# Pooled attention and MLP-mixer on one core: batch 0 is prepared in the way of the other batches

## The chip, the cores and the metric

The kernel runs on one core of one Trainium2 chip. Such a core has TensorE (matmuls, called PE in the profile; its weight loads are PEld), VectorE (DVE), ScalarE (ACT), GpSimd (POOL) and SyncE (SP); each works through its own list of instructions in order, and waits on semaphores where it needs what another one makes. Sixteen DMA engines move data between the chip's memory and the core's. The metric is the device time of one execution in microseconds (us); the median of several runs counts.

## What is computed

The reference, cut to what matters:

```python
# q, k, v: (8 batches, 8 heads, 576 rows, 64); x below is attention's output as (8, 576, 512)
k_p = k.reshape(B, H, 72, 8, D).mean(axis=3)          # keys pooled by 8 rows
v_p = v.reshape(B, H, 72, 8, D).mean(axis=3)          # values too
scores = (1 / sqrt(D)) * q @ k_p.transpose(0, 1, 3, 2)
attn = softmax(scores, axis=-1)
x = attn @ v_p                                        # heads side by side in 512 columns

h = relu(x.transpose(0, 2, 1) @ w_tok1) @ w_tok2      # 576 -> 256 -> 576
u = x + h.transpose(0, 2, 1)
out = u + relu(u @ w_ch1) @ w_ch2                     # 512 -> 1536 -> 512
```

All eight batches use the same weights. Inputs and output are fp32.

## The kernel before, in words

**Order.** Nothing is left to a scheduler: the whole program is recorded under `tc.manual_schedule`, and the order in which Python calls the steps is the order of instructions on every engine. Two texts at the top hold that order. `HEAD` is a list of tokens that are run first: loads (`L...`), dummy matmuls on a zeroed tile that feed nothing (`d4` is four of them), the attention of batch 0, and the first steps of batch 1. `PLAN` has one dictionary for each of nine units. A unit is the channel MLP of one batch (units 0 to 7; unit 8 takes the left-over rows of all batches): 12 tiles of the first product (`l1_tile`, lines L515 to L522, two steps each) and then seven products of 12 matmuls (L583, three steps each), whose sums and differences of operands (`=1` to `=4`, `w0` to `w3`, L545 and L557) are made by DVE. Between its steps `PLAN` puts the attention and token mixing of the next batches: `2.s0` is step `s0` of batch 2, `5.lq` a load of batch 5's queries, `g` a gate: a DVE memset and a POOL copy of one number (L716, L717) that keeps POOL from running ahead of that place.

**PSUM.** `take` and `give` hand out four one-bank tiles (p1a to p1d) in the order in which they come free. The pool `ps_two` has two tiles of two banks that are used in turn: a tile can be written again when the instruction that reads it has ended.

**A batch 1 to 7.** Its queries come with one POOL DMA as bf16, four heads on the 128 partitions, 18 rows of queries to a partition (`load_q`, L126). `qD` (steps `Q0`, `Q1`, L281) turns them on DVE by 32 x 32 blocks. Keys and values come with 72 partitions in use, eight rows to be pooled side by side (`kv`, L117). Keys are pooled by three adds (`pool8`, L171) on POOL, for batch 1 by eight accumulating matmuls with the identity (`kpool`, L250), and turned by four transposes on TensorE and a copy on ACT (`kpT`, L219). `scores` (L291, steps `s0` to `s2`) makes scores with 32-row matmuls on four row groups of the array at a time, into both `ps_two` tiles, and two exps on ACT. `av` (L372) multiplies with the values and normalizes on DVE (L383, L384); `at`, `u` and `t` are the token mixing.

**Batch 0** has steps of its own in `HEAD`. Queries of heads 0 to 3 come as fp32 with two SP DMAs (L742) and are cast by ACT and DVE (`c0`, `c1`, L694), those of heads 4 to 7 come with a POOL DMA (`Lq`, L700), 9 rows to a partition. `q0` to `q3` (`qT`, L272) turn two heads each by five transposes on TensorE and a DVE copy. Keys come with three POOL DMAs (`LkA`, `LkT`, `LkB`: heads 0 to 3, the last eight partitions, heads 4 to 7). `kp0` to `kp2` (`kp2`, L227) pool them by matmuls with the identity, DVE copies the sums into a zeroed tile (`kpz`), and `kt0` to `kt2` (`kt2`, L238) turn them, once for even and once for odd blocks of rows. `o0` to `o3` and `e0` to `e3` (`score`, L309) make the scores of two heads with full 128-row matmuls, one `ps_two` tile and one exp each. Then `vpool0` and `vpool1` (L259) pool the values on TensorE, `a00` to `a14` (`avh`, L325) multiply four heads with them and normalize on DVE (L338, L339), `m00` to `m14` (`ath`, L347) are the first product of the token mixing in two halves of columns, whose relu is one ACT instruction for the first half and an ACT and a DVE one for the second (L362, L364, L365), and `X0` to `X3` and `A0` to `A3` (L464, L472) make batch 0's turned input of the channel MLP. `1.kpool` pools batch 1's keys, `p0` and `p1` permute a weight (L159).

## Time and profile before

| | |
|---|---|
| runs of the kernel | 264.4, 265.07, 265.51 us; median 265.07 |
| the execution that was profiled | 264.03 us |
| its span, first to last instruction | 262.2 us |
| TensorE busy | 255.8 us (98%) |
| DVE, ACT, POOL busy | 179.7, 119.2, 150.0 us |
| TensorE, 0 to 6.55 / 6.55 to 13.10 / 13.10 to 24.10 us | 5.36 / 5.60 / 10.90 us busy |
| granted TensorE clock | 1.00 in the whole span |

How to read it: the profile gives each engine's instructions with their start and duration. A line such as `L517 PE MATMUL p1d<-uT,w_ch 128*128 128x512` is an instruction of line 517 on TensorE with 128 rows and 128 columns of weights, that writes tile p1d, 512 columns wide, from uT and w_ch. What stands in brackets or after `<-` behind it is the idle time of the engine before it, and what ended that. In the waits, the three numbers are us in total, how often, and the longest. Matmuls overlap each other, so their durations are longer than the time from one start to the next; 512 columns take 0.216 us from start to start. DMA landings are the start of the issue plus the time to landing that the trace gives.

### The profile page before, as it was taken

To read this page: it belongs to the slowest core of one execution; us is meant where nothing else is said; L and a number is where in the kernel's file an instruction comes from. 1 tells how busy PE (TensorE), PEld (TensorE's weight loads), DVE (VectorE), ACT (ScalarE), POOL (GpSimd) and SP (SyncE) were. 2 spreads that over 40 slices of the span, in tenths; PEclk is the share of its full clock that TensorE was granted. 3 is DMA by queue.
4 is the path that set the end of the run, shared out by engine and by line. 5 is a ranking of instruction groups with operands and counts; after the bars stand their busy time and mean duration, and the time that the engine had idled before them with its cause. 6 is when DMAs were issued, how large, how long until landed. Compare 5 with 4: busy or idle time off the path is not lost.

```text
span 262.2 us, 5324 instructions
## 1 busy us (share of the span) xinstructions
PE 255.8 (98%) x2121; PEld 160.4 (61%) x2121; DVE 179.7 (69%) x370; ACT 119.2 (45%) x195; POOL 150.0 (57%) x177
## 2 busy tenths in 40 slices
PE   8899999999999999999999999999999999999994
PEld 3775556754658545864487448744774486486483
DVE  4566489998786657993899449964795486175183
ACT  2445754149465554435641584155535502612610
POOL 8576145999989999999939881988000000101000
PEclk9999999999999999999999999999999999999999
DMA  7999999992096839699357840831414054503204
GB/s 150 191 200 205 206 206 208 207 223 77 2 172 101 133 118 201 146 196 261 66 154 125 239 133 2 162 92 41 123 35 127 5 158 113 129 0 88 75 0 160
DMA packets 31704, 34.29 MB, mean 131 GB/s; under 512 B 3136, under 2 KB 23744, under 8 KB 31680
## 3 DMA queue, kind: packets, MB, share of 16 engines
q0 software_dynamic: 17632, 17.64, 42.6%
q1 hardware_dynamic: 13632, 15.93, 20.4%
q10 hardware_dynamic: 416, 0.39, 0.5%
q8 instruction: 16, 0.26, 0.4%
q14 instruction: 8, 0.07, 0.1%
HBM read 38.99 MB, written 12.58 MB: 197 GB/s over the span
## 4 chain that ended last, share of the span: by engine, by line
PE 80%; POOL 8%; DMA 7%; DVE 3%; issue 1%; POOLq 0%
PE p1d L517 9%; PE p1c L517 9%; PE p1a L517 8%; PE p1b L517 7%; PE p1b L583 7%; PE p1c L583 7%; PE p1a L583 6%; DMA qb<-in_q_dram 5%; PE p1d L583 4%; PE p L297 3%; PE p L379 3%; POOL t L174 2%; POOL t L175 2%; DMA kr<-in_k_dram 2%; PE p L583 2%; PE p1d L393 2%
## 5 line engine op out<-in xcount | busy, mean ns | idle before, releaser
L717 POOL COPY flag<-flag 1x1 f32<-1x1 f32 x47 | 12.6, 269 | 94.5 <-DVE flag L716 94.5
L517 PEld LDWEIGHTS <-w_ch 128*128 128x128 bf16 x432 | 39.6, 98 | 43.4 <-issue 1.8
L583 PEld LDWEIGHTS <-area 128*128 128x128 bf16 x432 | 40.9, 98 | 7.4 <-issue 1.2
L306 ACT ACTIVATE ex<-p 72x768 bf16<-72x768 f32 x42 | 31.6, 803 | 15.9 <-PE p L297 15.7
L583 PEld LDWEIGHTS <-GT 128*128 128x128 bf16 x324 | 30.8, 98 | 8.2 <-issue 2.4
L175 POOL TENSOR_TENSOR t<-t 72x512 f32<-72x512 f32 x23 | 31.0, 1346 | 1.8
L521 ACT ACTIVATE GT<-p1d 128x512 bf16<-128x512 f32 x29 | 17.3, 597 | 27.0 <-PE p1d L517 21.4
L517 PE MATMUL p1d<-uT,w_ch 128*128 128x512 bf16 x104 | 28.8, 379 | 0.0
L174 POOL TENSOR_TENSOR t<-kr 72x1024 f32<-72x1024 bf16 x12 | 25.9, 2155 | 0.5
L517 PE MATMUL p1c<-uT,w_ch 128*128 128x512 bf16 x96 | 26.1, 379 | 0.0
L521 ACT ACTIVATE GT<-p1b 128x512 bf16<-128x512 f32 x26 | 15.6, 598 | 23.2 <-PE p1b L517 16.8
L517 PE MATMUL p1a<-uT,w_ch 128*128 128x512 bf16 x92 | 25.3, 379 | 0.0
L517 PE MATMUL p1b<-uT,w_ch 128*128 128x512 bf16 x92 | 24.2, 379 | 0.0
L174 POOL TENSOR_TENSOR t<-vr 72x1024 f32<-72x1024 bf16 x11 | 24.1, 2187 | 0.3
L521 ACT ACTIVATE GT<-p1a 128x512 bf16<-128x512 f32 x26 | 15.5, 596 | 11.8 <-PE p1a L517 9.2
L521 ACT ACTIVATE GT<-p1c 128x512 bf16<-128x512 f32 x27 | 16.1, 598 | 8.7 <-PE p1c L517 8.3
L384 DVE TENSOR_TENSOR x<-p,den 128x512 bf16<-128x512 f32 x28 | 19.4, 692 | 1.0
L557 DVE TENSOR_TENSOR area<-GT 128x1536 bf16<-128x1536 bf16 x9 | 9.8, 1086 | 12.4 <-ACT GT L521 12.4
L545 DVE TENSOR_TENSOR area<-GT 128x1536 bf16<-128x1536 bf16 x9 | 10.6, 1178 | 10.1 <-ACT GT L521 7.7
L379 PEld LDWEIGHTS <-ex 72*128 72x128 bf16 x280 | 13.4, 98 | 5.6 <-DVE flag L716 0.4
L583 PE MATMUL p1c<-area,area 128*128 128x256 bf16 x120 | 15.4, 273 | 0.0
L379 PE MATMUL p<-vp,ex 72*128 72x65 bf16 x280 | 14.6, 194 | 0.0
(188 smaller groups left out, 461.1 us busy)
## 6 DMA issues: line engine op xcount, KB each, us to landing
out_dram<-o SPq DMA_DIRECT2D x32, 256.0 KB, 4.0
qb<-in_q_dram POOLq DMA_DIRECT2D x7, 576.0 KB, 9.3
kr<-in_k_dram POOLq DMA_DIRECT2D x7, 512.0 KB, 7.4
vr<-in_v_dram POOLq DMA_DIRECT2D x7, 512.0 KB, 9.8
w_ch<-in_moe_w_ch_dram POOLq DMA_DIRECT2D x5, 512.0 KB, 15.8
mem<-u SPq DMA_DIRECT2D x10, 256.0 KB, 2.0
v<-mem SPq DMA_DIRECT2D x20, 128.0 KB, 2.8
area<-in_q_dram SPq DMA_DIRECT2D x2, 288.0 KB, 3.0
```

What stands on the lines that cost most here:

```text
L174: eng.tensor_tensor(out=t4[:, 0:n], in0=t[:, hs, 0:4], in1=t[:, hs, 4:8], op=ALU.add)
L175: eng.tensor_tensor(out=t4[:, 0:n, 0:2], in0=t4[:, 0:n, 0:2], in1=t4[:, 0:n, 2:4], op=ALU.add)
L297: nc.tensor.matmul(out=pss[l // 2][0:SP, l % 2, o:o + n1 - n0], lhsT=st["kD"][quad, g, db, :], rhs=st["qD"][quad, g, n0:n1, db], start=(db ...
L306: nc.scalar.activation(out=dst, in_=src, func=AF.Exp, scale=scale)
L379: nc.tensor.matmul(out=ps[:, h // 4, (h % 4) * (D + 1):(h % 4 + 1) * (D + 1)], lhsT=st["ex"][:, h * S + n0:h * S + n0 + P], rhs=st["vp"][: ...
L384: nc.vector.tensor_tensor(out=dst.rearrange("p (a h d) -> p a h d", a=2, d=D), in0=view[:, :, :, 0:D], in1=den[rows, :, :, None].broadcast ...
L517: nc.tensor.matmul(out=ps, lhsT=w_ch1[:, kk, m * P:(m + 1) * P], rhs=uT[kk], start=(kk == 0), stop=(kk == 3))
L521: nc.scalar.activation(out=GT[:, m, :], in_=ps, func=AF.Relu)
L545: nc.vector.tensor_tensor(out=out, in0=a, in1=b, op=ALU.subtract)
L557: nc.vector.tensor_tensor(out=S4[:, 0], in0=GT[:, f, hi], in1=GT[:, sec, hi], op=ALU.add)
L583: nc.tensor.matmul(out=ps[i] if split else ps[:, i], lhsT=chunk(u, i, a(m)), rhs=w(m), start=start and m == 0 and (i == 0 or split), stop= ...
L717: nc.gpsimd.tensor_copy(out=flag[:, 1:2], in_=flag[:, 0:1])
```

## The change

Batch 0 drops its own way and takes that of the other batches. Its queries all come by POOL, four heads to a DMA (`Lqa`, `Lqb`), and are turned by DVE (`Q0`, `Q1`). The keys of heads 0 to 3 come as fp32 by the SP queue (two DMAs, 64 and 8 partitions) into `kf` and are pooled by three DVE adds (`k0`); those of heads 4 to 7 come by POOL (`LkT` now has only these heads, `LkB` as before), are pooled by matmuls and copied by DVE (`kp2`). Each half is turned by two transposes and an ACT copy (`h0`, `h1`). Scores are `s0` to `s2`. Casts, `qT`, `kt2`, `score` and two memsets go. `HEAD` and `PLAN` are written anew; every unit keeps its kinds of matmuls, while places of steps, loads and gates differ.

```diff
-HEAD = """LkA LkT LkB Lq LvA LvT LvB Lt1 Lk1 Lt2 Lc1a Lq1 Lc1b Lc1c Lv1 Lc2b Lc1d p1 Lc2a Lc2c d4 c0 prep d3 c1 d4 d2 d1 q0 d2 kp0 kp1 kt0 q1 kt1 o0 kp2 o1 q3 e1 kt2 e0 q2 e3 vpool0 o3 d1 d1 a00 e2 vpool1 o2 a02 m01 d1 a04 m00 a12 m03 X1 m02 a10 m04 X0 p0 a14 1.kpool m11 m12 m14 m13 m10 A1 X3 A0 X2 A2 A3"""
+HEAD = """Lqa LkT LkB Lqb LvT LvA LvB Lt1 Lk1 Lt2 Lc1b Lc1a Lq1 Lc1c Lv1 Lc1d p1 Lc2a Lc2b Lc2c prep d4 d2 d3 k0 d3 d2 d4 h0 Q0 s0 kp2 Q1 h1 s1 vpool0 s2 vpool1 a00 a02 a04 m01 m00 X0 a10 X1 m03 m02 a12 m04 p0 1.kpool m10 m12 a14 m13 A1 X3 m11 m14 A0 X2 A2 A3"""
...
-    {2: "3.av4", 3: "3.av0 4.K0", 7: "3.av1", 8: "g 4.K1", 10: "3.av2 3.av3", 13: "g 3.at0", 14: "3.at1 g 6.lk", 16: "4.kpT", 17: "=3", 18: "4.Q0 3.u2", 19: "3.u1", 20: "3.u0", 21: "3.M0", 22: "3.u3 4.s2", 23: "3.M2 4.V1 3.u4", 24: "4.V0", 25: "=1", 26: "=2 3.M4", 27: "4.s0 g", 28: "6.lq", 30: "=4 g", 31: "4.s1 5.lv", 34: "3.M g", 35: "4.av2 3.T1", 36: "3.MT", 38: "3.T2", 40: "3.T3 3.T0", 41: "4.av4", 44: "5.lq 3.T5"},
...
+    {1: "4.K1", 2: "3.av4", 3: "3.av0", 7: "3.av2", 9: "4.K0", 10: "g 3.av1", 11: "3.av3", 12: "g =3", 14: "6.lk 3.at1", 15: "3.at0 g", 16: "4.Q0", 17: "4.V0 4.kpT", 18: "3.u1 3.u3", 20: "3.u0 4.V1", 21: "3.u2 4.s2", 22: "3.u4 3.M0", 24: "=1 3.M2", 25: "g 5.lq", 26: "=2", 27: "3.M4 4.s1", 28: "5.lv 6.lq", 31: "=4", 33: "6.lv", 35: "4.s0 3.M", 36: "3.T2 3.T3", 39: "3.T0 g 3.MT", 42: "3.T1 4.av2", 44: "4.av0"},
...
+    kf = area2[0:SP, 0:2 * HP * POOL * D].bitcast(FP32).rearrange("j (h i d) -> j h i d", i=POOL, d=D)
...
-        h0, h1, j0, j1 = {"A": (0, HP, 0, BP), "B": (HP, H, 0, BP), "T": (0, H, BP, SP)}[part]
+        h0, h1, j0, j1 = {"A": (0, HP, 0, BP), "B": (HP, H, 0, BP), "T": (HP * (key == "k"), H, BP, SP)}[part]
...
+    def q_group(b, g):
+        return q[b, 4 * g:4 * g + 4].rearrange("l (j n) d -> (l j) (n d)", n=2 * BR)
...
+        def kpT_half(g):
+            def go():
+                ps = take([P, 2, SP], BF16)
+                for e in range(2):
+                    nc.tensor.transpose(out=ps[:, e, :], in_=st["kp"][:, g, e].rearrange("j l d -> j (l d)"),
+                                        identity=ident[0:SP, 0:SP])
+                nc.scalar.copy(out=st["kD"][:, g], in_=ps)
+                give(ps)
+            return go
...
+        def kp_sbuf():
+            pool8(nc.vector, kf, slice(0, HP), st["kp"][:, 0], True)
+
+        def kp_psum():
+            ps = take([P, 512], FP32)
+            for i in range(POOL):
+                nc.tensor.matmul(out=ps[0:SP, 0:HP * D], lhsT=ident[0:SP, 0:SP], rhs=loaded[b, "k"][:, HP:H, i, :],
+                                 start=(i == 0), stop=(i == POOL - 1))
+            nc.vector.tensor_copy(out=st["kp"][:, 1].rearrange("j e l d -> j e (l d)"),
+                                  in_=ps[0:SP, 0:HP * D].rearrange("j (n e) -> j e n", e=2))
+            give(ps)
...
+            name[f"h{g}"] = kpT_half(g)
+        name["k0"], name["kp2"] = kp_sbuf, kp_psum
...
-    def late_q():
-        nc.gpsimd.dma_start(out=loaded[0, "q"][:, 2:HP, 0:BR * D], in_=q_pairs(2, HP))
+    def first_q(g):
+        nc.gpsimd.dma_start(out=quarters(loaded[0, "q"])[:, g], in_=q_group(0, g))
...
-        for a in range(2):
-            nc.sync.dma_start(out=qf[:, a:a + 1, :], in_=q_pairs(a, a + 1))
+        for j0, j1 in ((0, BP), (BP, SP)):
+            nc.sync.dma_start(out=kf[j0:j1].rearrange("j h i d -> j h (i d)"),
+                              in_=k[0, 0:HP].rearrange("h (j i) d -> j h (i d)", i=POOL)[j0:j1])
...
-        nc.vector.memset(qb[:, :, BR * D:], 0.0)
-        nc.vector.memset(kpz, 0.0)
```

## The prediction

> **What bounds the kernel now.** I read four views, in this order: the busy shares of the page, the waits, the timeline of the first 25 us, and the groups by shape.

> ```profile
> span 262.2 us, 5324 instructions
> PE 255.8 (98%) x2121; PEld 160.4 (61%) x2121; DVE 179.7 (69%) x370; ACT 119.2 (45%) x195; POOL 150.0 (57%) x177
> PE   8899999999999999999999999999999999999994
> PEclk9999999999999999999999999999999999999999
> DMA  7999999992096839699357840831414054503204
> ```

> TensorE is full from the third of 40 slices to the last but one, and the DMA engines are full in slices 2 to 9. So the span is a head that ends when the first matmul of unit 0 can go, a body in which TensorE streams, and a tail. Only two kinds of change count: the head's end, and waits of TensorE in the body. The waits say how few of these there are; DVE's wait for a query load is the cause of the largest.

> ```profile
> PE p1a L683 <- DVE area L740: 1.2, 1, 1.2
> PE p1d L232 <- DMA kr<-in_k_dram: 0.9, 1, 0.9
> PE p1c L415 <- DVE u L416: 0.4, 1, 0.4
> ...
> DVE qD L284 <- DMA qb<-in_q_dram: 4.3, 1, 4.3
> ```

> The timeline gives the dates of the head.

> ```profile
> 4.38 0.46 DVE L694 CAST qb<-area 128x576 bf16<-128x576 f32 x1 [1.37 <-DMA area<-in_q_dram]
> 10.79 0.70 POOL L118 DMA_DIRECT2D kr<-in_k_dram  x1 [1.09 <-DMA qb<-in_q_dram]
> 16.43 0.21 DVE L338 RECIPROCAL den<-p 128x8 f32<-128x8 f32 x1 [0.88 <-PE p L333]
> 18.72 0.59 POOL L118 DMA_DIRECT2D vr<-in_v_dram  x1 [1.38 <-DMA kr<-in_k_dram]
> 19.18 1.89 PE L253 MATMUL p1b<-kr,ident 72*72 72x512 bf16 x8
> 24.18 0.59 PE L517 MATMUL p1c<-uT,w_ch 128*128 128x512 bf16 x2
> ```

> The SP queue's 576 KB had landed at 4.4, batch 0's last queries at 10.5, batch 1's keys at 18.6. Pooling those (`1.kpool`) starts at 19.18, and from there TensorE runs without a gap: 8 x 0.216 for kpool, ten 256-column matmuls of the second half of `m` (1.07), X3 and X2 (0.45), A0 to A3 (1.73) make 4.98, and 19.18 + 4.98 = 24.16, against 24.18 seen. Work before 19.18 matters only if it moves that start.

> **The change, removed.** TensorE loses kp0 and kp1 (0.44 + 0.45), sixteen key transposes (0.6), twenty query transposes (4 x 0.28) and sixteen score matmuls (2.0): some 4.6 us. DVE loses copies (4 x 0.49, 0.29 + 0.29, 0.31 + 0.30 + 0.46), a cast of 0.46 and two memsets (0.17 + 0.70); ACT a cast of 0.67 and eight exps (5.15). All of it lies before 19.18, so by itself it is worth nothing.

> **Added.** The rows of the later batches give the prices.

> ```profile
> 27.43 0.54 PE L297 MATMUL p<-qD,kD 32*72 32x384 bf16 x8
> 28.00 1.50 ACT L306 ACTIVATE ex<-p 72x768 bf16<-72x768 f32 x2 [0.73 <-PE p L297]
> ...
> L284 DVE STREAM_TRANSPOSE qD<-qb 128x576 uint32<-128x576 uint32 x14 | 10.5, 762 | 5.1 <-DMA qb<-in_q_dram 4.3 <-issue 0.9
> L174 DVE TENSOR_TENSOR t<-vr 72x1024 f32<-72x1024 bf16 x1 | 2.2, 2221 | 0.0
> L175 DVE TENSOR_TENSOR t<-t 72x512 f32<-72x512 f32 x1 | 1.1, 1105 | 0.0
> ```

> Three score steps cost TensorE 0.46 each, plus 0.31 for going into and out of row groups (0.10 + 0.22 beyond the columns, the same at every such place): 2.3. Their exps take ACT 3 x 1.50 = 4.5. Two query transposes take DVE 0.76 each. h0 and h1 are two key transposes each (0.07) and an ACT copy of at most 0.40 (L224, twice as wide); they lie beside Q0 and Q1 and end before them. Pooling fp32 keys on DVE (k0) is not in the trace. Lower bound: adds of two inputs with 512 and 256 fp32 results (L626) take 0.68 and 0.41, so 1.36 + 0.68 + 0.41 = 2.45. Upper bound: the one pooling that DVE does, for batch 2, takes 2.22, 1.10 and 2.23, 5.55 in all, while POOL runs adds of its own. In the head POOL only issues DMAs, and DVE adds beside DMA issues (L545 at 43.35 to 45.3) keep their 0.96, so I take 2.45.

> The loads hold the same bytes in the same places: SP 576 KB fp32 before and after; POOL's first four DMAs 1,728 KB as read, both times. So the last queries still land at 10.5, the first half of them where keys came in at 6.96 with 64 KB less, so 7.1, and batch 1's keys at 18.6. What is new is that SP writes fp32 to 72 partitions and not to 128. Early bound: 4.4, as the queries. Late bound: the key load of 64 partitions, 256 KB as written, landed 1.30 after the one ahead of it, 201 GB/s; the first 288 KB of queries landed 2.9 after issue, of which 0.7 is transfer (the second landed 0.7 behind), so 0.74 + 2.2 + 2.9 for 576 KB = 5.9. The key load has the shape, so I take 5.9 and keep 4.4. [...]

> **The chain after the change**, dates for 5.9, and for 4.4 in brackets. k0 ends at 8.4 (6.9); Q0, behind it on DVE, at 9.2 (7.95, after the landing at 7.1). s0 runs at 9.25, its exps 0.55 later, until 11.3 (10.0). kp2 is queued behind s0 on TensorE, its cast ends at 11.2 (10.3), and Q1 is queued behind that cast on DVE: 12.0 (11.3, by the landing at 10.5). s1 at 12.05, exps 12.6 to 14.1 (11.95 to 13.45). s2 needs the two PSUM tiles of s1; the second comes free with the last exp, so its exps run 14.65 to 16.15 (14.05 to 15.55). a00 takes the first tile at 15.45, DVE normalizes until 16.85; a02 the second, until 17.8 (17.25; 0.93 each, as at 14.62 and 16.43). X0's last chunks wait for that: 17.85. Then X0, a10, X1, m03, m02, a12 and m04 add 1.5 to 1.6, and kpool starts at 19.45 (18.85) against 19.18. It can't start before 18.61. Behind it stand the 4.98 and a14 (0.15), now after kpool, and about 0.2 for A2, since the second half of AT goes through ACT (0.38) and then DVE (0.42), and m14 is now queued five steps later: 24.8 (24.2). So the head gains nothing, though its exps end 0.6 to 1.2 earlier: **+0.6 us (0.0)**. The removed first wait for keys is replaced by one for exps and PSUM tiles.

> **Body.** Every unit's list keeps the matmuls; steps move between neighbours. By start-to-start times in the body, real waits are 0.30 (47.1), 0.30 (56.1), 0.61 (124.6) and some 0.1: 1.3. The 0.61 goes: batch 5's queries were issued at 111.08, behind batch 6's, and landed at 123.28. Now they stand at step 25 of unit 2, not 44, and ahead: issue at about 107, landing near 115, wanted near 121. What is late next is batch 6's: about 122.5 (three loads of 2.9 and the stores between), wanted near 124. POOL's pooling for 2.kpT still starts behind the sixth subtraction or addition of unit 0, at 46, so the 0.30 there stays. Bounds: -1.3, all gone; +1.5, as much again in new places. I take **-0.6**. Tail: the same, 0.

> Sum: +0.6 - 0.6 = 0. The profiled execution took 264.03, its span 262.2 and 1.8 around it; the median of the runs is 265.07, 1.04 more. So the span stays 262.2, and the forecast is **265.1**.

> **Rivals.**
> 1. Faster: keys land at 4.4, kpool goes at once with its load (19.18 to 18.61 at best, less 0.35 for a14 and A2, so -0.2), and all body waits go (-1.3): 263.6. For it: dense TensorE is all that is left. Against: it needs everything at its best, and the page has no more to give.
> 2. Slower, k0 on DVE costs 5.55: every date from Q0 on slips by 3.1, since k0 over 1.8 already pushes Q1 past its landing. 265.1 + 3.1 = 268.2; with keys at 4.4, 266.6. For it: DVE's only rows of this pooling. Against: POOL was adding then.
> 3. Slower, the clock. TensorE has dummies until about 6.9, then works some 2.4 of the next 5.7 us (h0, s0, kp2, h1, s1), where the view by windows shows it busy for 5.6 of the 6.55 us to 13.1. The first dummies, with nothing before them, start 0.43 apart, those from 4.8 on 0.216, though the page's clock row has a 9 from the first slice. Should that half rate come back at about 11 and last as long as at the start (3.7), s1, vpool0, s2, vpool1 and a00 take twice their time, 1 to 2 us of it on the chain: 266.6. It decides from where a gap is long enough; before, 1.1 us (6.6 to 7.7) was not. [...]
> 4. Slower, the rewritten plan brings new waits of 1.5 to 2 us, batch 6's queries the likeliest: 266.8.

> **Chances.** Forecast, within 0.5% (1.3 us, about what a measurement can tell from no change): 0.55. Rival 1: 0.13. Rival 2: 0.11. Rival 3: 0.10. Rival 4: 0.11. So faster 0.13, same 0.55, slower 0.32. The range goes from 263.6, rival 1, to 267.3, which takes in rivals 3 and 4 and the early form of 2.

> **What would show it.** First L517 at 24.2 to 24.8; L174 on the new keys 1.4 long, starting near 5.9; exps of s1 starting right behind Q1; kpool near 19.4 behind a02's normalization; all PEclk at 9; no wait of qD for qb near 119. Wrong if kpool starts after 20, if the granted clock falls, or if a wait over 1 us stands in the body.

## The result and the profile after

The changed kernel takes **271.4 us** (median of six runs, 270.45 to 275.05), the kernel before 264.8 (six runs, 263.47 to 265.51). The ratio is 1.0244, with a 95% interval of 1.021 to 1.0279: slower by 6.6 us, where no change was forecast. The profiled execution took 271.25, its span 269.5. Ratios, here and below, leave out runs that are over 1.5% above the fastest of their kernel: the one of 275.05 here, three of the seven of e3_both.

The page of the changed kernel, with the rows that were shown of the kernel before (40 slices of 6.74 us):

```profile
span 269.5 us, 5255 instructions
...
PE 260.2 (97%) x2088; PEld 161.0 (60%) x2088; DVE 176.5 (65%) x363; ACT 118.4 (44%) x194; POOL 151.3 (56%) x177
...
PE   8589999999999999999999999999999999999994
...
PEclk9755999999999999999999999999999999999999
```

TensorE executes 33 matmuls fewer and is busy 4.4 us longer. The clock row tells why before any instruction is looked at: a 7 and two 5s where the kernel before had 9s, and a hole (5) in TensorE's row above the 7. The view by windows puts numbers on it (length; busy us and instructions of PE, PEld, DVE, ACT, POOL; granted clock; packet time over 16 DMA engines, which can pass 1; GB/s):

```profile
0.00:6.55 6.55, 5.36 (x13) 1.90 (x14) 1.21 (x8) 1.28 (x1) 5.43 (x14) 1.00 0.71 144
6.55:13.10 6.55, 3.82 (x22) 1.75 (x21) 3.02 (x4) 1.30 (x3) 3.42 (x7) 0.80 1.35 188
13.10:19.65 6.55, 5.56 (x43) 3.40 (x42) 1.53 (x3) 3.19 (x6) 4.71 (x7) 0.50 1.38 183
19.65:26.20 6.55, 5.96 (x60) 5.07 (x59) 3.37 (x10) 0.95 (x2) 4.27 (x6) 0.50 1.26 206
26.20:32.75 6.55, 6.49 (x45) 3.69 (x44) 3.51 (x8) 3.04 (x5) 2.30 (x4) 0.89 1.25 205
```

A mean of 0.80 in the second window is half rate in 40% of it, that is from 10.5; 0.89 in the last is half rate in 22% of it, until 27.6. So TensorE ran at half rate for 17 us. (The trace's clock events say 10.52 and 27.59. The first event is at 7.11; the view counts the time before it as full, though the dummies start 0.43 apart there.) In the first 13 us only the second window differs in work: TensorE is busy for 3.8 us there, against 5.6 before.

The waits name the hole (us in total, times, longest):

```profile
DVE t L170 <- DMA area<-in_k_dram: 6.0, 1, 6.0
...
PE p1c L217 <- DVE kp L174: 2.4, 1, 2.4
```

TensorE's first wait for keys (0.9 before) is now one of 2.4 for VectorE's pooled keys, and VectorE waited for the keys of the SP queue. The 4.3 us that `qD` waited for a query load are gone:

```profile
L267 DVE STREAM_TRANSPOSE qD<-qb 128x576 uint32<-128x576 uint32 x16 | 11.9, 760 | 0.1
...
L170 DVE TENSOR_TENSOR t<-area 72x1024 f32<-72x1024 f32 x1 | 1.2, 1222 | 6.0 <-DMA area<-in_k_dram 6.0
```

The timeline has the dates that the prediction set (start, duration, in brackets the idle time before):

```profile
7.13 1.03 PE L648 MATMUL p1b<-area 128*128 128x512 bf16 x4
...
8.05 1.22 DVE L170 TENSOR_TENSOR t<-area 72x1024 f32<-72x1024 f32 x1 [5.98 <-DMA area<-in_k_dram]
9.31 0.69 DVE L171 TENSOR_TENSOR t<-t 72x512 f32<-72x512 f32 x1
10.03 0.42 DVE L174 TENSOR_TENSOR kp<-t 72x256 bf16<-72x256 f32 x1
10.37 0.77 DVE L267 STREAM_TRANSPOSE qD<-qb 128x576 uint32<-128x576 uint32 x1
...
11.20 0.86 PE L280 MATMUL p<-qD,kD 32*72 32x384 bf16 x8 [0.38 <-DVE qD L267]
...
11.98 1.92 PE L237 MATMUL p1d<-kr,ident 72*72 72x256 bf16 x8
...
26.07 2.64 PE L246 MATMUL p1c<-kr,ident 72*72 72x512 bf16 x8
...
32.19 0.59 PE L482 MATMUL p1d<-uT,w_ch 128*128 128x512 bf16 x2
```

The first product of unit 0 (L482, formerly L517) starts at 32.19 against 24.18: the head is **8.0 us longer**. From there to the end it is 269.5 - 32.19 = 237.3, against 262.2 - 24.18 = 238.0: the body is **0.7 shorter**. So all of the loss lies ahead of 32.19. Two things went another way there than predicted: `k0` starts at 8.05 and not at 5.9, and the clock falls. `kp2` (L237) takes 1.92 where it took 1.06 at the full rate (e7_one_gap).

### The profile page after: what moved, and what is told of

Its sections match the earlier page's. It is cut to its first block, busy times and chain, and to the rows that moved or that the text cites. A ratio compares the mean times of both kernels' runs of the same rounds, so it can differ in the third digit from the quotient of the medians.

```text
span 269.5 us, 5255 instructions
## 1 busy us (share of the span) xinstructions
PE 260.2 (97%) x2088; PEld 161.0 (60%) x2088; DVE 176.5 (65%) x363; ACT 118.4 (44%) x194; POOL 151.3 (56%) x177
## 4 chain that ended last, share of the span: by engine, by line
PE 85%; DVE 6%; POOL 4%; DMA 2%; issue 1%; SPq 0%; ACT 0%; POOLq 0%; DVEq 0%
PE p1c L482 9%; PE p1d L482 9%; PE p1a L482 8%; PE p1b L482 7%; PE p1a L548 7%; PE p1d L548 7%; PE p1c L548 6%; PE p1b L548 5%; PE p L280 5%; PE p L346 3%; PE p1a L360 2%; DMA area<-in_k_dram 2%; PE p1b L382 2%; PE p L548 2%; POOL t L170 2%; DVE area L510 1%
## 5 line engine op out<-in xcount | busy, mean ns | idle before, releaser
L482 PEld LDWEIGHTS <-w_ch 128*128 128x128 bf16 x432 | 39.5, 98 | 43.9 <-issue 2.7
L679 POOL COPY flag<-flag 1x1 f32<-1x1 f32 x47 | 15.6, 331 | 82.9 <-DVE flag L678 82.9
L289 ACT ACTIVATE ex<-p 72x768 bf16<-72x768 f32 x48 | 36.0, 801 | 21.1 <-PE p L280 21.1
L482 PE MATMUL p1c<-uT,w_ch 128*128 128x512 bf16 x112 | 29.9, 379 | 0.0
L486 ACT ACTIVATE GT<-p1c 128x512 bf16<-128x512 f32 x31 | 18.5, 597 | 24.1 <-PE p1c L482 20.5
L482 PE MATMUL p1d<-uT,w_ch 128*128 128x512 bf16 x100 | 27.6, 379 | 0.0
L482 PE MATMUL p1a<-uT,w_ch 128*128 128x512 bf16 x88 | 23.7, 379 | 0.0
L482 PE MATMUL p1b<-uT,w_ch 128*128 128x512 bf16 x84 | 22.2, 379 | 0.0
L351 DVE TENSOR_TENSOR x<-p,den 128x512 bf16<-128x512 f32 x28 | 19.4, 691 | 1.0
L486 ACT ACTIVATE GT<-p1b 128x512 bf16<-128x512 f32 x24 | 14.3, 597 | 10.7 <-PE p1b L482 6.2
L522 DVE TENSOR_TENSOR area<-GT 128x1536 bf16<-128x1536 bf16 x9 | 8.7, 963 | 12.6 <-ACT GT L486 12.5
L280 PE MATMUL p<-qD,kD 32*72 32x384 bf16 (+1 forms) x256 | 13.8, 313 | 0.9 <-DVE qD L267 0.9
L383 DVE TENSOR_TENSOR u<-p1a,x 128x512 bf16<-128x512 f32 x8 | 5.8, 730 | 12.9 <-PE p1a L382 12.7
```

The source lines that it names most:

```text
L280: nc.tensor.matmul(out=pss[l // 2][0:SP, l % 2, o:o + n1 - n0], lhsT=st["kD"][quad, g, db, :], rhs=st["qD"][quad, g, n0:n1, db], start=(db ...
L289: nc.scalar.activation(out=dst, in_=src, func=AF.Exp, scale=scale)
L351: nc.vector.tensor_tensor(out=dst.rearrange("p (a h d) -> p a h d", a=2, d=D), in0=view[:, :, :, 0:D], in1=den[rows, :, :, None].broadcast ...
L383: nc.vector.tensor_tensor(out=rows_of(c), in0=blocked(ps), in1=blocked(x), op=ALU.add)
L482: nc.tensor.matmul(out=ps, lhsT=w_ch1[:, kk, m * P:(m + 1) * P], rhs=uT[kk], start=(kk == 0), stop=(kk == 3))
L486: nc.scalar.activation(out=GT[:, m, :], in_=ps, func=AF.Relu)
```

## The experiments

Theory: the late keys and the clock both count, the clock most. The late keys open the hole between the last dummy (8.2) and `h0` (10.5), and the hole drops the clock. Rivals: the late keys alone set the date and the clock costs nothing on the chain; or the new way of batch 0 is simply longer; or the new plan is at fault. In this list "first product" is the start of the first matmul of unit 0, and ratios are to runs of the kernel before on the same chip, with their 95% intervals.

| kernel | us (runs) | ratio | `k0` starts | first product | rest of the span |
|---|---|---|---|---|---|
| before | 264.8 (6) | | | 24.18 | 238.0 |
| changed | 271.4 (6) | 1.0244 [1.021, 1.0279] | 8.05 | 32.19 | 237.3 |
| e1_dummies | 266.81 (4) | 1.009 [1.0066, 1.0115] | 8.42 | 27.70 | 237.3 |
| e2_tail_first | 272.24 (4) | 1.0305 [1.0271, 1.0338] | 7.62 | 32.54 | 237.4 |
| e3_both | 267.25 (7) | 1.0073 [1.0046, 1.01] | 7.67 | 26.71 | 237.6 |
| e4_old_way_new_plan | 263.75 (12) | 0.9962 [0.9941, 0.9983] | | 24.07 | 237.3 |
| e5_act_tail_dummies | 265.35 (10) | 1.0035 [1.0015, 1.0056] | 5.91 | 26.80 | 237.3 |
| e6_act_tail | 269.84 (4) | 1.0186 [1.0112, 1.026] | 5.90 | 30.75 | 237.3 |
| e7_one_gap | 269.41 (4) | 1.0204 [1.0164, 1.0245] | 8.17 | 30.03 | 237.3 |
| e8_repaired | 264.28 (12) | 0.9986 [0.9966, 1.0006] | 5.88 | 24.70 | 237.3 |
| e9_old_way_act | 263.64 (12) | 0.9974 [0.995, 0.9997] | | 24.34 | 237.4 |

**The clock alone.** Dummies in `HEAD` wherever TensorE waits; nothing else changes.

```diff
-h0 Q0 s0 kp2 Q1 h1 s1 vpool0 s2 vpool1 a00 a02 a04
+d11 h0 Q0 d2 s0 kp2 d4 Q1 h1 d2 s1 vpool0 d2 s2 vpool1 d3 a00 d2 a02 d2 a04
```

> The changed kernel with 28 more dummy matmuls in TensorE's waits of the head (11 before h0, 2 before s0, 4 behind kp2, 2 behind h1, 2 behind vpool0, 3, 2 and 2 around a00 and a02); loads and everything else as changed. Clock theory (the half clock from 10.5 to 27.6 is the bulk of the loss, and it came because TensorE had no work): the granted clock stays 1.00, kpool starts near 21.4 and the first matmul of unit 0 near 26.7, since the SP keys still land at 8; time 266 to 267. Theory of the late keys (the chain behind the landing at 8 makes the loss, the clock is a side effect): the first matmul stays near 30 and the time near 270, whatever the clock.

The clock stays full and the first product comes 4.5 earlier, although TensorE is given 28 matmuls more:

```profile
8.42 1.22 DVE L170 TENSOR_TENSOR t<-area 72x1024 f32<-72x1024 f32 x1 [6.35 <-DMA area<-in_k_dram]
...
14.39 0.53 PE L280 MATMUL p<-qD,kD 32*72 32x384 bf16 x8
...
22.33 1.89 PE L246 MATMUL p1c<-kr,ident 72*72 72x512 bf16 x8
...
27.70 0.59 PE L482 MATMUL p1d<-uT,w_ch 128*128 128x512 bf16 x2
```

So the clock is on the chain, and the larger part of the loss. The time is within what was expected; the first product comes 1.0 later than the 26.7 expected, with keys that are 0.4 later still (8.42). What is left, 27.70 against 24.18, begins with those late keys.

**The order of the two key loads.** The small one (8 partitions, 64 KB) goes first.

```diff
-        for j0, j1 in ((0, BP), (BP, SP)):
+        for j0, j1 in ((BP, SP), (0, BP)):
```

> The changed kernel with the two SP loads of keys in the other order, the eight partitions first, the 64 behind them; no dummies added. If the small load was late because it had to share the DMA engines with POOL's loads, all SP keys land near 6 and k0 starts there, 2 us earlier. Theory of the late keys: the time falls by 2 us for the dates and by more if the clock holds, 264 to 266. Clock theory: it depends on whether a window of 3.4 us that is some 60% full, then one of 45%, keeps the clock; if it falls, at 10.5 or 13.9, the time is 269 to 270.5, if it holds, 264.5 to 266.

A miss: now the large load is the late one, landing at 7.5 and not near 6, and `k0` gains 0.43. The clock falls here too, later (at 12.95), and 272.24 lies above every time that was expected:

```profile
7.62 1.22 DVE L170 TENSOR_TENSOR t<-area 72x1024 f32<-72x1024 f32 x1 [5.54 <-DMA area<-in_k_dram]
...
10.07 0.24 PE L217 MATMUL p1c<-ident,kp 72*128 72x72 bf16 x2 [2.40 <-DVE kp L174]
```

Whichever of these two loads stands second in SP's queue is late.

**Both.** That order, and 16 dummies.

```diff
-h0 Q0 s0 kp2 Q1 h1 s1 vpool0 s2 vpool1 a00 a02 a04
+d2 h0 Q0 d2 s0 kp2 d3 Q1 h1 d2 s1 vpool0 d2 s2 vpool1 d2 a00 d1 a02 d2 a04
...
-        for j0, j1 in ((0, BP), (BP, SP)):
+        for j0, j1 in ((BP, SP), (0, BP)):
```

> Both edits: the eight partitions first, and 16 more dummies in TensorE's waits. Clock theory with early keys: clock 1.00, kpool near 19.4, first matmul of unit 0 near 24.8, as the prediction had it, and a body 0.7 shorter than before: 264.4, within 0.5% of before. If the prediction's chain was wrong in itself, the first matmul comes after 25.5 with a clock of 1.00.

In the profiled run the clock held, and the first product came at 26.71. But of seven runs four took 266.0 to 267.3 and three 271.2 to 272.1, these with a mean clock of 0.975. So sixteen dummies in these places do not hold the clock in every run.

**The plan alone.** The old way of batch 0 with the new `PLAN`.

```diff
-PLAN = [ ... of the kernel before
+PLAN = [ ... of the changed kernel
```

> The kernel before, with the nine dictionaries of the changed kernel's PLAN and its own HEAD: what the rewritten plan alone does. Prediction: 0.6 us less, 264.2 against 264.8, by the wait for batch 5's queries that goes. Rival: the new plan has waits of its own, 1 us or more slower.

263.75, and 237.3 from the first product on, as in the changed kernel. The plan is worth 0.7 in the trace and 1.0 in the ratio (264.8 x 0.0038; the interval reaches from 0.45 to 1.6). The rival that blames the plan is out.

**The small key load on another queue.** ScalarE's queue issues it beside the large one on SP's; with the dummies of e1_dummies, and without any.

```diff
-        for j0, j1 in ((0, BP), (BP, SP)):
-            nc.sync.dma_start(out=kf[j0:j1].rearrange("j h i d -> j h (i d)"),
+        for eng, j0, j1 in ((nc.sync, 0, BP), (nc.scalar, BP, SP)):
+            eng.dma_start(out=kf[j0:j1].rearrange("j h i d -> j h (i d)"),
```

> The changed kernel with the 28 dummies of e1_dummies, and the small key load (8 partitions, 64 KB) issued by ScalarE's queue beside the large one on SP's, not behind it. Theory A: the pooling on VectorE starts at 8.0 to 8.4 because the small load is queued behind 512 KB; then it lands by 6, the pooling starts near 6.0 and ends near 8.5, Q0 waits for its load (8.2 to 8.7) and s0 runs near 9.6 instead of 11.56, s1 is held by the second query load (11.1 to 11.6) and runs near 12.5 instead of 14.39; the first product of unit 0 comes near 25.8 instead of 27.70: about 264.9 us. Rival B: the small load is late because POOL's loads take the DMA engines or the same partitions; then it lands near 8 again, or the large one slips, and the time stays at 266.8.

`k0` starts at 5.91, the date of the prediction; both of batch 0's query loads also land earlier, by 2.1 and 1.5 (6.56 and 10.08, against 8.67 and 11.57 in e1_dummies). Now the eleven dummies ahead of `h0` stand in the way (`kp` is ready near 8.3, `h0` runs at 10.07), so the first product gains only 0.9 and not 1.9:

```profile
5.91 1.22 DVE L170 TENSOR_TENSOR t<-area 72x1024 f32<-72x1024 f32 x1 [3.84 <-DMA area<-in_k_dram]
...
10.07 0.23 PE L217 MATMUL p1d<-ident,kp 72*128 72x72 bf16 x2
...
26.80 0.59 PE L482 MATMUL p1d<-uT,w_ch 128*128 128x512 bf16 x2
```

> The same move of the small key load, without any dummy added. Theory A with the clock as the traces have it so far (half rate after a window of 3.41 us with 26% work, or after two of 40%): with keys at 6 the gap of 2.35 us between the last dummy (8.0) and h0 closes, the window from about 7 to 10.5 holds 50 to 60% work and the clock stays: 265 to 266 us. Theory A with a stricter clock (half rate below some 60% work): 269 to 270. Rival B (the load is late for another reason): the gap stays, the clock falls as in the changed kernel, 271.4 us.

Without dummies the dates up to the fall are nearly those predicted (9.25 for `s0`), but the clock falls all the same:

```profile
8.35 0.24 PE L217 MATMUL p1c<-ident,kp 72*128 72x72 bf16 x2 [1.61 <-DVE kp L174]
...
9.04 0.53 PE L280 MATMUL p<-qD,kD 32*72 32x384 bf16 x8 [0.45 <-DVE qD L267]
...
11.86 0.86 PE L280 MATMUL p<-qD,kD 32*72 32x384 bf16 x8 [0.47 <-DVE qD L267]
...
30.75 0.59 PE L482 MATMUL p1d<-uT,w_ch 128*128 128x512 bf16 x2
```

Between `s0` at 9.04 and `s1` at 11.86 the same kind of group goes from 0.53 to 0.86: the fall shows in the durations as well as in the clock row. Keys in time did not save the clock, which was the hope of "theory A with the clock as the traces have it"; 269.84 is what the stricter clock gave (269 to 270). One of the four runs took 267.07 at a mean clock of 0.980, the others 269.8 to 270.6 at 0.966 to 0.968, so the fall does not last equally long in every run.

**One gap.** Eleven dummies ahead of `h0`, none elsewhere.

```diff
-d4 h0 Q0 s0
+d4 d11 h0 Q0 s0
```

> The changed kernel with eleven dummies ahead of h0 and none elsewhere: only the gap of 2.35 us is filled. Theory C: that gap alone dropped the clock; then it is full all through, and the time is that of e1_dummies or up to 0.8 below it, since 17 dummies on the chain are gone: 266.0 to 266.9 us, first product of unit 0 at 27.0 to 27.7. Rival D: the sparse stretch behind it drops the clock too (h0, s0, kp2, s1 and s2 without dummies keep TensorE busy for some 40 to 55% of 10.5 to 14): then half rate from about 14 for four to five windows of 3.41 us, 269 to 271 us.

Rival D has it, with half rate for three windows where four to five were expected. The view by windows (second to fourth):

```profile
6.55:13.10 6.55, 5.77 (x35) 2.67 (x33) 3.24 (x5) 1.50 (x3) 3.23 (x7) 1.00 1.34 183
13.10:19.65 6.55, 5.76 (x49) 3.97 (x50) 1.31 (x3) 3.69 (x7) 4.90 (x7) 0.57 1.38 183
19.65:26.20 6.55, 5.96 (x59) 4.58 (x57) 4.00 (x10) 1.58 (x3) 4.19 (x5) 0.65 1.26 205
```

The fall comes later (0.57 in the third window: 86% of it at half rate, from 14.0), after a stretch in which no single wait of TensorE was longer than 0.6. The long gap was not needed for it.

**Both terms repaired.** The small load on ScalarE's queue, and 18 dummies only where e6_act_tail shows TensorE waiting (the expectation says 19; the places that it lists, and the edit, make 18).

```diff
-h0 Q0 s0 kp2 Q1 h1 s1 vpool0 s2 vpool1 a00 a02 a04
+d7 h0 d1 Q0 s0 kp2 d2 Q1 h1 d2 s1 vpool0 d2 s2 vpool1 d1 a00 d2 a02 d1 a04
...
-        for j0, j1 in ((0, BP), (BP, SP)):
-            nc.sync.dma_start(out=kf[j0:j1].rearrange("j h i d -> j h (i d)"),
+        for eng, j0, j1 in ((nc.sync, 0, BP), (nc.scalar, BP, SP)):
+            eng.dma_start(out=kf[j0:j1].rearrange("j h i d -> j h (i d)"),
```

> The changed kernel with both failed terms repaired: the small key load on ScalarE's queue, and 19 dummies placed where e6_act_tail shows TensorE waiting (seven ahead of h0, one ahead of Q0, two after kp2, two after h1, two after vpool0, one after vpool1, two after a00, one after a02). If late keys and the clock are all that went wrong, the chain is the one predicted: keys at 5.9, s0 near 9.0, s1 near 11.9, first product of unit 0 at 24.5 to 24.8, span near 262, 263.6 to 264.1 us. If the chain from s1 on is longer than predicted, as in e1_dummies and e5_act_tail_dummies (13.3 us from s1 to the first product, where 12.75 was predicted), the first product comes at 25.2 and the time is 264.4. If the clock still falls: 268 to 270.

```profile
span 262.0 us, 5266 instructions
...
PEclk9999999999999999999999999999999999999999
```

```profile
5.88 1.22 DVE L170 TENSOR_TENSOR t<-area 72x1024 f32<-72x1024 f32 x1 [3.81 <-DMA area<-in_k_dram]
...
9.02 0.54 PE L280 MATMUL p<-qD,kD 32*72 32x384 bf16 x8 [0.23 <-DVE qD L267]
...
11.84 0.53 PE L280 MATMUL p<-qD,kD 32*72 32x384 bf16 x8 [0.32 <-DVE qD L267]
...
14.46 1.50 ACT L289 ACTIVATE ex<-p 72x768 bf16<-72x768 f32 x2 [0.55 <-PE p L280]
...
19.34 1.89 PE L246 MATMUL p1c<-kr,ident 72*72 72x512 bf16 x8
...
24.70 0.59 PE L482 MATMUL p1d<-uT,w_ch 128*128 128x512 bf16 x2
```

This is the chain on record, date by date: `s0` 9.25 predicted and 9.02 seen, `s1` 12.05 and 11.84, exps of `s2` 14.65 and 14.46, `kpool` 19.45 and 19.34, first product 24.8 and 24.70, span 262.2 and 262.0, time 265.1 and 264.28. The median of 264.28 is 0.2 above the range that was expected, the first product within its own. So late keys and the fallen clock are the whole loss: with both mended, the new way of batch 0 costs 24.70 - 24.18 = 0.5 in the head, the plan gives 0.7 back in the body, and the kernel cannot be told from the one before.

**The old way with the other queue.** e4_old_way_new_plan, with the second of its first query loads on ScalarE's queue.

```diff
-            nc.sync.dma_start(out=qf[:, a:a + 1, :], in_=q_pairs(a, a + 1))
+            (nc.scalar if a else nc.sync).dma_start(out=qf[:, a:a + 1, :], in_=q_pairs(a, a + 1))
```

> The old way of batch 0 with the new plan (e4_old_way_new_plan), and the second of its two first query loads on ScalarE's queue. If the second place in SP's queue costs a load its date, as for the small key load, that load lands earlier than 5.21, but the end of the head is set by batch 1's keys (landing at 18.3) and by what stands ahead of their pooling, so 263.4 to 263.9 us. If POOL's loads come earlier too, as in e6_act_tail, by some 0.3: 263.3.

The load lands at 4.35, not 5.21. That does not show that the queue did it: in the kernel before, with the same two loads on SP's queue, it landed at 4.36, so this date differs by 0.85 between two traces of the same loads. (The small key load is steadier: `k0` starts at 8.05, 8.42 and 8.17 with it second in SP's queue, and at 5.91, 5.90 and 5.88 with it on ScalarE's.) Nothing comes of it either way, since batch 1's keys (18.88) still end the head. 263.64, the same as e4_old_way_new_plan within their intervals; by the ratios the two are 0.26% and 0.38% faster than the kernel before.

## Why the prediction was wrong, step by step

- **"So I take 5.9 and keep 4.4" (keys by the SP queue): half wrong.** The large load landed at 5.71, as estimated. The estimate added the bytes of both loads at the rate of one; the small load, issued at 1.56, landed at 7.95 by its semaphore events and held `k0` until 8.05. Mis-sized by 2.1 us. Mended alone it gives 32.19 - 30.75 = 1.4, mended under a full clock 27.70 - 24.70 = 3.0 (some of that is dummies of e1_dummies that stood on the chain).
- **Query landings, 7.1 and 10.5: late by 1.1 and 0.6** (8.22 and 11.13). With the small load on ScalarE's queue, 6.65 and 10.16.
- **k0 at 2.45 and not 5.55: right** (8.05 to 10.45, 2.40). Rival 2 falls.
- **The prices of exps and transposes: right**, as e8_repaired shows, and the chain built from them within 0.25 at each date. The price of row groups was too high: in the trace before, a score step stands 0.09 behind the columns ahead of it, and the 0.46 that it takes already holds the 0.14 behind its own columns. So three steps cost 3 x 0.55, some 1.7, and not 2.3. No date of the chain uses the difference.
- **Body -0.6: right**, -0.7 in the changed kernel, -0.4 to -0.7 in every experiment, all of which have the new plan. The wait for batch 5's queries is gone, and so is one of the two of 0.30; in the changed kernel one wait is left, of 0.41 at 64.4, ahead of the transposes of keys that POOL pools. Rival 4 falls, and so does rival 1: no run with the new way of batch 0 ended its head before 24.70.
- **The clock, rival 3 at 0.10: this step failed.** The prediction saw the mechanism and its place ("should that half rate come back at about 11"; it came back at 10.5), and then put it at 0.10 by the length of gaps: 1.1 us had not dropped the clock in the trace before, but no run shows a length up to which it stays. That was the wrong measure, and so was the price: "last as long as at the start (3.7)". It lasted 17.07. At the start the half rate meets a stream of dummies, here it met the sparse work that had called it. The gap itself was longer than the 1.1 before, 2.35 from the last dummy's end to `h0`, since the keys were late; but with the keys in time (e6_act_tail) the clock fell as well, at 11.07.

What the traces show instead: clock changes lie multiples of 3.413 us apart (7.11, 10.52, 27.59 in the changed kernel: 3.413, then 17.067, five times that), and the falls go with the share of such a window in which TensorE has columns to work on, not with its longest gap. The shares are worked out from the matmuls in the traces, at 0.427 us for 512 columns at half rate, as seen from start to start, and half of that at the full rate (with the 0.216 seen there, a share grows by two points at most, those below 50% by one):

| trace | window ahead of the fall | its share | half rate lasts | lowest window of the head without a fall |
|---|---|---|---|---|
| before | none | | | 66% |
| changed | 7.11 to 10.52 | 26% | 17.07 | |
| e2_tail_first | 9.54 to 12.95 | 39% | 17.07 | 40% |
| e6_act_tail | 7.66 to 11.07 | 38% | 17.07 | 67% |
| e7_one_gap | 10.56 to 13.97 | 39% | 10.24 | 94% |
| e1_dummies, e3_both, e8_repaired | none | | | 54%, 50%, 71% |
| e4_old_way_new_plan, e5_act_tail_dummies, e9_old_way_act | none | | | 79%, 81%, 81% |

The rate fell after windows of 26 to 39%, and stayed after those of 50% and more; a single one of 40% (e2_tail_first) did not drop it. In the changed kernel it did not come back after windows of 72, 62, 91 and 76%, only after one of 99% (in e2_tail_first and e6_act_tail after the second such one, in e7_one_gap after one of 94%). The share of one window does not settle the way back either: in e6_act_tail 90% brought the full rate at the start (0.84 to 4.25), and 95% did not later (14.49 to 17.90). The longest wait of TensorE does not tell the falls apart from the rest: the clock fell behind one of 2.4 (changed) and, in e7_one_gap, after a stretch with none above 0.6, and it stayed through one of 0.9 in the kernel before.

Two points stay open. One is where the bound lies, and what else decides at it: 39% dropped the rate and 40% once did not, which is no difference that this working can tell, and no trace has a window at the full rate between 40 and 50%. The windows begin at another place in every run (the first full-rate one between 4.25 and 7.15), which would explain why e3_both fell in three of its seven runs, but those three have no trace. The other is why the second load of SP's queue is late. The semaphore events have the small load landing at 7.95 there, at 3.41 by ScalarE's queue (e6_act_tail) and at 3.27 first in SP's queue (e2_tail_first). Second in the queue, its packets run from 4.7 to 6.3, behind those of the large load and beside POOL's: from 4.6 to 6.8 the DMA view counts 275 packets of POOL's queue and 48 of SP's. By ScalarE's queue they run from 1.7 to 2.3, before any of POOL's. Whether the 512 KB ahead or POOL's loads beside it cost more, no run separates.

## What to carry to other kernels

A rewritten head should be priced with TensorE's share of each 3.4 us, and not with its longest gap alone: the new way takes some 2.7 us of work off TensorE (an estimate: the 4.6 that go, less 1.7 for the score steps and 0.14 for the key transposes) and has its dummies all ahead of the keys, and that left windows of 26 to 39% in which the clock fell. In e8_repaired 18 dummies placed where TensorE waits cost the chain nothing that shows (first product at 24.70, 24.8 predicted), while the eleven ahead of `h0` in e5_act_tail_dummies held it until 10.07, against 8.35 without them (e6_act_tail). For two loads that one engine waits for, two queues are worth a trial: here `k0` gained 2.1 us by them, in the old way nothing. A date taken from the sum of their bytes was only a lower bound here.
